# Order of the opening loads and orientation of the last expert's products in a fused attention and expert kernel

## The chip, the core and the metric

The kernel runs on one core of one Trainium2 chip. The metric is the device time of one execution in microseconds, as the median of several runs. The inputs lie in the chip's memory before the run and the output is written back to it. "fp32r" below is a float32 format that TensorE multiplies in one pass; a plain float32 product takes two.

## The reference, cut to what matters

Gated linear attention (4 sequences, 8 heads, 768 steps, head size 48), then a feed-forward layer with a rational gate (384 to 2048 to 384), then a mixture of four experts (each 384 to 1024 to 384), whose outputs are summed with normalised probabilities per token:

```python
f = 1.0 / (1.0 + np.exp(-f_logit))
for t in range(S):
    state = f[:, :, t, :, None] * state + einsum('bhd,bhe->bhde', k[:, :, t], v[:, :, t])
    y[:, :, t] = einsum('bhd,bhde->bhe', q[:, :, t], state)
...
h = x @ w_in
P = a[0] + a[1] * h + a[2] * h**2 + a[3] * h**3
Q = 1.0 + abs(b[0]) * abs(h) + abs(b[1]) * h**2
x = (P / (Q + 1e-06)) @ w_out
...
p = domain_probs / (domain_probs.sum(-1, keepdims=True) + 1e-09)
for e in range(E):
    out += p[:, e:e + 1] * (np.maximum(x @ w1[e], 0.0) @ w2[e])
```

## The kernel before, in words

Time is cut into six chunks of 128 steps. A chunk has four blocks, one per sequence, each of 128 tokens with all heads; a chunk therefore is 512 tokens. The chunks go through attention, feed-forward layer and experts as a pipeline: while TensorE multiplies chunk c by the experts' weights, the other engines prepare chunk c+1. The order on each engine is the order in which the program issues its instructions, and nothing is reordered by a scheduler.

**The opening.** `Att.start` queues, on SyncE, the loads of the first two blocks (f, k, q by `Block.load`, L415; v by `load_v`, L420) and then calls `fetch` three times. `fetch` (L726) loads one pair of raw slots: two slots of the feed-forward layer's weights, in a 64-bit format, 768 KB each. Then `Att.first(s, conv)` runs once for each s from 0 to 4. For the new block s it computes the gate sums: `exp` of f on ScalarE (L424, issued one round ahead), `w` (L428) and four `scans` on VectorE (L435), `inverse` on ScalarE, which is a logarithm and an exponential (L440, L441), then `k_hat` (L446), `newton1`, `newton2` (L451, L456) and `q_hat` (L461) on VectorE, and on TensorE `scores` (L465) and the key transposes `k_t` (L481). For the old block s-1 it runs `k_copy` (the transposed keys out of a bank on ScalarE, L485), `masked` (L476), the outputs (L489), `update` (L523), `x_hi` (L532) and `finish` (L547). In each round from s = 1 on, `conv` turns a raw slot into float32 weights: two passes on ScalarE (L738, L739), two on VectorE (L741, L742) and an addition (L745), after which the result is stored (L754) and, after every second slot, the next pair is fetched. At its end a round queues the f, k, q loads of block s+2 and the v load of block s+1; a block's tiles have two buffers, so a load waits until the block two before has been read.

**The fill.** After the fourth block the feed-forward products of chunk 0 run (`fill_in` L880, `fill_out` L887). From there on TensorE is fed without pause until the end.

**The experts.** A step v takes one slot of one expert: `mm_in` (L842) multiplies 128 hidden features by 512 tokens, nine products of 128x128 weights with 512 columns; ScalarE and VectorE split the result after the relu into a high and a low part (`gh` L950, `gl` L951); a step later `mm_out` (L852) adds the slot's share to three banks `acc`, each holding 128 features by 512 tokens, again with nine products of 512 columns. After the eight slots of an expert `evac2` multiplies the three banks by the token's probability (L987, VectorE) and adds them to the sum `o` (L988, GpSimd). A finished chunk is turned by `write_out`: for each block of 128 tokens three transposes of `o` into a bank (L1012), a copy on ScalarE (L1019) and a DMA to the output (L1021). For the last expert of the last chunk `end` does the multiplication and addition on VectorE in halves (L968, L969), then calls `write_out` for all four blocks.

Of the kernel before, what the change touches and what calls it, by code (L numbers as in the profile page):

```python
# [8 lines left out]
F32 = mybir.dt.float32  # L9
# [4 lines left out]
ALU = mybir.AluOpType  # L14
# [3 lines left out]
NB, NH, S, D = 4, 8, 768, 48  # L18
DM = NH * D
C = 128  # L20
NCH = S // C
NP = NH // 2
PR = 112
NE = 4
NJ1 = 16
NJ2 = 8
# [312 lines left out]
LAST = NCH * NE * NJ2  # L339
# [213 lines left out]
class Att:  # L553
# [24 lines left out]
    def start(self, fetch):  # L578
        nc = self.tc.nc
        for b in range(NB):  # L580
            nc.gpsimd.memset(self.st[b], 0.0)
        for b in range(2):
            blk = self.blocks[0, b] = Block(self, 0, b)
            for i in (2, 1, 0):
                blk.load(i)
            blk.load_v()
        for _ in range(3):
            fetch()

    def warm(self, n):  # L590

# [1 line left out]
        for _ in range(n):  # L593
            self.tc.nc.tensor.matmul(self.spare[:, 0:C], ident, ident, start=True, stop=True)

    def first(self, s, conv):

        new, old, nxt = (self.blocks.get((0, b)) for b in (s, s - 1, s + 1))
        rs = range(NP)
        if s == 0:  # L600
            new.exp()
            self.warm(WARM[0])
        if old:
            old.k_copy()
        if new:
            new.w()
            new.scans()
            new.inverse()
            new.k_hat()
        if nxt:  # L610
            nxt.exp()
        for f in conv[0]:
            f()
        if old:
            old.masked()
            for f in old.y_parts():
                f()
            for r in rs:
                old.update(r)
        if new:  # L620
            new.newton1()
            new.newton2()
            new.q_hat()
        if old:
            old.x_hi()
        if new:
            self.warm(WARM[1])
            for r in rs:
                new.scores(r)
            for r in rs:  # L630
                new.k_t(r)
            self.warm(WARM[2])
        for f in conv[1]:
            f()
        if old:
            old.finish()
        if s + 2 < NB:
            blk = self.blocks[0, s + 2] = Block(self, 0, s + 2)
            for i in (2, 1, 0):
                blk.load(i)  # L640
        if old and s + 1 < NB:
            self.blocks[0, s + 1].load_v()

    def loads(self, v):
        for c in range(1, NCH):
# [43 lines left out]
def fused(ctx, tc, aps, consts, gm, big, dp, prep, flag_op):  # L689


    nc = tc.nc
    w1, w2, out = aps["w1"], aps["w2"], aps["out"]
    sc, pn, ident, mask = consts

    pp = ctx.enter_context(tc.tile_pool(name="pp", bufs=1, space=PSUM))
    banks = [pp.tile([128, 512], F32, name=f"bank{i}") for i in range(8)]
    acc, hb, h1 = banks[0:3], banks[3:5], banks[5]

    def pool(name, bufs):  # L700
        return ctx.enter_context(tc.tile_pool(name=name, bufs=bufs))
# [144 lines left out]
    def mm_out(pairs, start, stop):  # L846
        for m in range(3):
            o = slice(m * 128, (m + 1) * 128)
            n, last = 0, 3 * len(pairs) - 1
            for (wh, wl), (gh, gl) in pairs:  # L850
                for a, b in ((wh, gh), (wl, gh), (wh, gl)):
                    nc.tensor.matmul(acc[m], a[:, o], b, start=(start and n == 0), stop=(stop and n == last))  # L852
                    n += 1
                    fill_step()

    def run_bounds(v):

        return (v % NJ2 == 0 or v in groups), ((v + 1) % NJ2 == 0 or v + 1 in groups)

    def emit(item):  # L860
        kind, what = item
        ts = take(len(halves(item)))
        if kind == "in2":
            c = where2(what)[0]
            mm_in(hb[what % 2], ts[0], x2[c])
        elif kind == "in1":
            c, j = what
            mm_in(h1, ts[0], att.x[c])
            gate_queue.append((c, j, h1))
        elif kind == "out2":  # L870
            mm_out([(ts[0], act2.pop(what))], *run_bounds(what))
        else:
            c, n = what
            mm_out([(ts[i], act1.pop((c, 4 * n + i))) for i in range(4)], True, True)
        make_ready(state["used"] + R)
# [85 lines left out]
    def end():  # L961

        c = NCH - 1
        for h in range(2):
            s = slice(256 * h, 256 * h + 256)
            for m in range(3):
                t = tp.tile([128, 512], F32, tag="t", name="t")
                nc.vector.tensor_tensor(out=t[:, s], in0=acc[m][:, s], in1=pb[c][:, NE - 1, s], op=ALU.mult)  # L968
                nc.vector.tensor_tensor(out=o[c][:, m, s], in0=o[c][:, m, s], in1=t[:, s], op=ALU.add)  # L969
            for b in range(2 * h, 2 * h + 2):  # L970
                write_out(c, b, banks[4 + b])

    def evac2(v):
        c, e, j = where2(v)
# [35 lines left out]
    def write_out(c, b, bank):  # L1010
        for m in range(3):
            nc.tensor.transpose(bank[:, m * C:(m + 1) * C], o[c][:, m, b * C:(b + 1) * C], ident)  # L1012
        if c < NCH - 1:
            t = osp.tile([128, DM], F32, tag="os", name="os")
        else:
            if b == 0:
                last.append(sp.tile([128, 3, 512], F32, tag="s1", name="os"))
            t = last[0].rearrange("p m t -> p (m t)")[:, b * DM:(b + 1) * DM]
        nc.scalar.copy(out=t, in_=bank[:, 0:DM])  # L1019
        r0 = b * S + c * C  # L1020
        nc.sync.dma_start(out=out[r0:r0 + C, :], in_=t)  # L1021
# [12 lines left out]
    for v in range(-FILL - 6, LAST + 1):  # L1034
        tau = v + FILL
        ops = att.begin(v)
        if tau == -4:
            prep()
        if tau + 6 <= NB:
            att.first(tau + 6, conv_ops(tau) if tau + 6 < NB else [[], []])  # L1040
        run_late()
        store_all()
        items = steps.get(v, [])
        lead = 1 if items and items[0][0] == "in2" and items[0][1] == v + 1 else 0
        fill_run(ops[PA], 9 * lead)
        for item in items[:lead]:
            emit(item)
        if 0 <= v < LAST and v not in act2:
            relu(v)
        for f in ops[ACT0]:  # L1050
            f()
        for u in gate_queue:
            if u[0] and u[:2] not in gate:
                gate[u[:2]] = gate_in(u)
        if 0 <= tau + 1 < NJ1:
            fill_in(tau + 1)
        ready = [u for u in gate_queue if u[:2] in gate]
        new = ready[0] if ready else None
        if new:
            gate_queue.remove(new)  # L1060
        old, pend_old = pend_old, new
        if new or old:
            gate_step(new, old, ops)
        else:
            for f in ops[DVE1] + ops[ACT1] + ops[POOL1]:
                f()
        c, k = v // (NE * NJ2) - 1, v % (NE * NJ2)
        if 0 <= c < NCH - 1 and k == 2:
            for b in range(2):
                write_out(c, b + (2 if c else 0), banks[6 + b])  # L1070
        fill_run(ops[PB], 9 * any(item[0] == "out2" for item in items), True)
        for item in items[lead:]:
            if item[0] == "out2":
                emit(item)
                if run_bounds(v - 1)[1]:
                    evac2(v - 1)
        for item in items[lead:]:
            if item[0] == "in2":
                emit(item)
                if v + 1 < LAST:  # L1080
                    relu(v + 1)
        if 0 <= c < NCH - 1 and k == (1 if c else 2):
            for b in range(2):
                write_out(c, b + (0 if c else 2), banks[6 + b])
        for item in items[lead:]:
            if item[0] == "out1":
                emit(item)
        for item in items[lead:]:
            if item[0] == "in1":
                emit(item)  # L1090
        for u in gate_queue:
            if not u[0] and u[:2] not in gate:
                gate[u[:2]] = gate_in(u)
        if tau == -1:
            spread_probs()
        if 0 <= tau - 2 < NJ1:
            fill_out(tau - 2)
        for f in ops[REST]:
            f()
        if v in groups:  # L1100
            evac1(*groups[v])
        if tau + 6 >= NB:
            for f in sum(conv_ops(tau), []):
                f()
            run_late()
        if 10 <= tau and v < -1:
            make_ready(min(R - 6, 2 * (tau - 9)))
            split_to(min(AHEAD, state["ready"] - 2))
        if tau == NJ1 + 1:
            for m in range(3):  # L1110
                split_x2(0, m, acc[m], nc.vector)
            load_pb(0)
        if v >= -1:
            split_to(state["used"] + AHEAD)
        att.loads(v)
        if v == 170:
            flag_op(banks[6], banks[7])
# [178 lines left out]
```

## Time and profile before

| | |
|---|---|
| median of 3 runs | 1397.06 us (1396.53 to 1398.14) |
| the profiled execution: its own time | 1395.27 us |
| the profiled execution: span on the core | 1393.5 us |
| TensorE busy, share of the span | 96% |
| VectorE, ScalarE, GpSimd busy | 64%, 48%, 21% |
| DMA, mean rate over the span | 209 GB/s |
| granted TensorE clock, mean | 0.985 of full speed |

The table says that TensorE is occupied for nearly the whole span. What is left over lies at the two ends: in the first of 40 equal slices (34.8 us each) TensorE is busy for 4 tenths, in the second for 7 tenths, in the last for 7 tenths, and in all between for 8 or 9. Times inside a profile are counted in us from the start of the span.

### The profile page before, as it was taken

The numbers are of one execution on the slowest core, as the hardware profiler recorded it, in microseconds if no ns is written. First come the engines' busy times: TensorE is split into PE (matmuls) and PEld (weight loads), VectorE is DVE, ScalarE is ACT, GpSimd is POOL, SyncE is SP. The second block draws the span as 40 slices with busy tenths as digits, with TensorE's granted clock in tenths as the row PEclk, the third lists the DMA queues.
The fourth block names the chain that finished last, engine by engine and source line by source line (L and its number), as shares of the span: only waits on it lengthen the run. The fifth ranks groups of instructions, "written<-read, shape, count | busy, mean of one in ns | idle before, by whom it ended". The sixth has DMA issues, their size and how long they took to land.

```text
span 1393.5 us, 19540 instructions
## 1 busy us (share of the span) xinstructions
PE 1335.1 (96%) x7134; PEld 1060.5 (76%) x7134; DVE 889.1 (64%) x1375; ACT 665.3 (48%) x1152; POOL 290.5 (21%) x257
## 2 busy tenths in 40 slices
PE   4799999899899999999999999999999999999997
PEld 4544787677678888877888877888888888888886
DVE  5899747697947666757666676566675556552222
ACT  3688437676626535534554435454454453431111
POOL 0133554566530010112001111001111001111010
PEclk8999999999999999999999999999999999999998
DMA  7546876667875656656755647566557566657660
GB/s 271 201 172 213 282 257 222 216 219 254 311 267 184 213 181 200 217 180 220 223 190 182 213 159 264 194 205 215 188 175 254 179 209 193 193 193 240 193 186 26
DMA packets 115704, 291.03 MB, mean 209 GB/s; under 512 B 13104, under 2 KB 28816, under 8 KB 114832
## 3 DMA queue, kind: packets, MB, share of 16 engines
q1 hardware_dynamic: 115024, 289.51, 62.8%
q8 instruction: 59, 0.97, 0.3%
q14 instruction: 45, 0.37, 0.1%
q10 hardware_dynamic: 576, 0.18, 0.1%
HBM read 240.83 MB, written 48.81 MB: 208 GB/s over the span
## 4 chain that ended last, share of the span: by engine, by line
PE 79%; DVE 13%; ACT 3%; DMA 2%; issue 1%; POOL 0%; SPq 0%; ACTq 0%; DVEq 0%; POOLq 0%
PE bank L852 36%; PE bank L842 33%; PE bank L887 3%; PE bank L880 3%; PE bank L489 2%; PE bank L465 1%; DVE q L916 1%; DVE g L435 1%; DMA f<-in_qkf_dram 1%; DVE q L925 1%; DVE y L935 1%; DVE y L937 1%; DVE q L911 1%; DVE q L913 1%; DVE gl L951 1%
## 5 line engine op out<-in xcount | busy, mean ns | idle before, releaser
L842 PE MATMUL bank<-x,w 128*128 128x512 f32 x2448 | 604.5, 394 | 11.3 <-DVE gl L951 9.1
L842 PEld LDWEIGHTS bank<-x,w 128*128 128x128 f32 x2448 | 457.3, 189 | 107.9 <-DVE gl L951 11.6
L852 PE MATMUL bank<-gh,w 128*128 128x512 f32 x1632 | 516.8, 396 | 6.6 <-DVE t L987 6.6
L852 PEld LDWEIGHTS bank<-gh,w 128*128 128x128 f32 x1632 | 302.8, 189 | 73.3 <-DVE t L987 7.4
L852 PE MATMUL bank<-gl,w 128*128 128x512 f32 x816 | 320.6, 393 | 0.0
L951 DVE SCALAR_TENSOR_TENSOR gl<-bank,gh 128x512 fp32r<-128x512 f32 x192 | 131.4, 685 | 153.0 <-ACT gh L950 152.5
L988 POOL TENSOR_TENSOR o<-o,t 128x512 f32<-128x512 f32 x69 | 89.0, 1319 | 549.4 <-DVE t L987 549.4
L852 PEld LDWEIGHTS bank<-gl,w 128*128 128x128 f32 x816 | 153.9, 189 | 33.1
L950 ACT ACTIVATE gh<-bank 128x512 fp32r<-128x512 f32 x192 | 113.6, 593 | 130.7 <-PE bank L842 130.7
L916 DVE SCALAR_TENSOR_TENSOR q<-q,sc,r 128x512 f32<-128x512 f32 x80 | 62.4, 780 | 152.3 <-ACT r L901 152.3
L799 POOL TENSOR_TENSOR w<-rawbuf,w 128x384 fp32r<-128x384 f32 x96 | 108.0, 1151 | 93.5 <-ACT w L798 77.5
L927 ACT CAST gh<-q 128x512 fp32r<-128x512 f32 x80 | 49.2, 615 | 159.0 <-DVE q L925 158.9
L896 ACT COPY h<-bank 128x512 f32<-128x512 f32 x80 | 46.8, 585 | 127.7 <-PE bank L842 127.2
L1005 DVE TENSOR_TENSOR s<-s,bank 128x512 f32<-128x512 f32 x45 | 30.6, 681 | 74.1 <-PE bank L852 74.1
L942 DVE TENSOR_TENSOR gl<-q,gh 128x512 fp32r<-128x512 f32 x80 | 56.0, 700 | 31.4 <-ACT gh L927 31.3
L917 ACT ACTIVATE r<-q,sc 128x512 f32<-128x512 f32 x80 | 58.0, 725 | 31.0 <-DVE q L916 24.2
L911 DVE SCALAR_TENSOR_TENSOR q<-q,r 128x512 f32<-128x512 f32 x80 | 65.7, 821 | 0.0
L902 ACT ACTIVATE y<-h,sc 128x512 f32<-128x512 f32 x80 | 64.2, 803 | 0.0
L435 DVE TENSOR_TENSOR_SCAN g<-f,sc 112x128 f32<-112x128 f32 x96 | 63.3, 719 | 0.5
L925 DVE SCALAR_TENSOR_TENSOR q<-y,sc,q 128x512 f32<-128x512 f32 x80 | 62.5, 781 | 1.8
L918 ACT ACTIVATE r<-r 128x512 f32<-128x512 f32 x96 | 60.8, 633 | 3.0
L937 DVE SCALAR_TENSOR_TENSOR y<-y,sc,h 128x512 f32<-128x512 f32 x80 | 60.1, 752 | 2.8
(103 smaller groups left out, 1216.4 us busy)
## 6 DMA issues: line engine op xcount, KB each, us to landing
w<-ws SPq DMA_DIRECT2D x448, 384.0 KB, 3.6
ws<-w SPq DMA_DIRECT2D x96, 384.0 KB, 4.0
raw<-in_w_dram SPq DMA_DIRECT2D x16, 768.0 KB, 6.9
rawbuf<-in_w_dram SPq DMA_DIRECT2D x64, 192.0 KB, 3.6
v<-in_v_dram SPq DMA_DIRECT2D x24, 320.0 KB, 4.7
f<-in_qkf_dram SPq DMA_DIRECT2D x24, 256.0 KB, 3.6
k<-in_qkf_dram SPq DMA_DIRECT2D x24, 256.0 KB, 4.1
q<-in_qkf_dram SPq DMA_DIRECT2D x24, 256.0 KB, 4.4
```

The costliest lines, as they stand in the source:

```text
L435: self.nc.vector.tensor_tensor_scan(g[:, r], f[:, r], lim, 1.0, ALU.mult, ALU.min)
L799: nc.gpsimd.tensor_tensor(out=t[:, 1], in0=r, in1=t[:, 0].bitcast(F32), op=ALU.subtract)
L842: nc.tensor.matmul(ps, a[:, o], b[:, kk, :], start=(n == 0), stop=(n == 8))
L852: nc.tensor.matmul(acc[m], a[:, o], b, start=(start and n == 0), stop=(stop and n == last))
L902: nc.scalar.activation(out=y, in_=h, func=AF.Identity, scale=sc[:, 0:1], bias=sc[:, 1:2])
L911: vec.scalar_tensor_tensor(out=q0, in0=q0, scalar=QC, in1=r0, op0=ALU.add, op1=ALU.mult)
L916: vec.scalar_tensor_tensor(out=q, in0=q, scalar=sc[:, 5:6], in1=r, op0=ALU.mult, op1=ALU.add)
L925: vec.scalar_tensor_tensor(out=q0, in0=y0, scalar=sc[:, 3:4], in1=q0, op0=ALU.subtract, op1=ALU.mult)
L937: vec.scalar_tensor_tensor(out=y, in0=y, scalar=sc[:, 2:3], in1=h, op0=ALU.subtract, op1=ALU.mult)
L950: nc.scalar.activation(out=gh, in_=h, func=AF.Relu)
L951: nc.vector.scalar_tensor_tensor(out=gl, in0=h, scalar=0.0, in1=gh.bitcast(F32), op0=ALU.max, op1=ALU.subtract)
L988: nc.gpsimd.tensor_tensor(out=o[c][:, m], in0=o[c][:, m], in1=t, op=ALU.add)
```

## The change

Three edits. (1) `start` fetches one pair of raw slots instead of three; the second pair is fetched at the end of round 0, behind the loads of the third block's f, k, q, and the third pair at the end of round 1, behind the fourth block's f, k, q and the third block's v. (2) In a round, `k_copy` of the old block is issued behind the new block's gate sums and `inverse` instead of ahead of them. (3) For the last expert of the last chunk the products are formed token by feature: the activations are the weights of the array, the expert's weights stream as 384 columns, and four banks hold 128 tokens by 384 features each. The sum of the first three experts is transposed and copied four and three steps before the last; at the end VectorE multiplies a bank by the probability of its tokens, adds the copied sum, and the DMA follows.

```diff
@@ start
-        for _ in range(3):
-            fetch()
+        fetch()
@@ first
-        if old:
-            old.k_copy()
         if new:
             new.w()
             new.scans()
             new.inverse()
             new.k_hat()
+        if old:
+            old.k_copy()
...
         if old and s + 1 < NB:
             self.blocks[0, s + 1].load_v()
+        if s + 2 < NB:
+            fetch()
@@ fused
     acc, hb, h1 = banks[0:3], banks[3:5], banks[5]
+    tok = acc + [h1]
...
+    def mm_tokens(w, g, start, stop):
+        (wh, wl), (gh, gl) = w, g
+        for b in range(NB):
+            o = slice(b * C, (b + 1) * C)
+            for n, (a, m) in enumerate(((gh, wh), (gh, wl), (gl, wh))):
+                nc.tensor.matmul(tok[b][:, 0:DM], a[:, o], m, start=(start and n == 0), stop=(stop and n == 2))
+                fill_step()
...
-            mm_out([(ts[0], act2.pop(what))], *run_bounds(what))
+            if what >= LAST - NJ2:
+                mm_tokens(ts[0], act2.pop(what), *run_bounds(what))
+            else:
+                mm_out([(ts[0], act2.pop(what))], *run_bounds(what))
@@ end
-        for h in range(2):
-            s = slice(256 * h, 256 * h + 256)
-            for m in range(3):
-                t = tp.tile([128, 512], F32, tag="t", name="t")
-                nc.vector.tensor_tensor(out=t[:, s], in0=acc[m][:, s], in1=pb[c][:, NE - 1, s], op=ALU.mult)
-                nc.vector.tensor_tensor(out=o[c][:, m, s], in0=o[c][:, m, s], in1=t[:, s], op=ALU.add)
-            for b in range(2 * h, 2 * h + 2):
-                write_out(c, b, banks[4 + b])
+        for b in range(NB):
+            t = last[0][:, b]
+            nc.vector.scalar_tensor_tensor(out=t, in0=tok[b][:, 0:DM], scalar=pn[:, c * NB + b, NE - 1:NE], in1=t,
+                                           op0=ALU.mult, op1=ALU.add)
+            r0 = b * S + c * C
+            nc.sync.dma_start(out=out[r0:r0 + C, :], in_=t)
@@ the loop over steps v, ahead of out2
+        if v in (LAST - 4, LAST - 3):
+            for b in range(2):
+                write_out(NCH - 1, b + 2 * (v - LAST + 4), banks[6 + b])
```

**Order on SyncE, from the first block's v load on.** `raw` are the raw slots; f, k, q and v belong to the second, third and fourth block in turn. Before:

```order
L420 DMA v<-in_v_dram 128x640
L415 DMA f<-in_qkf_dram 128x512
L415 DMA k<-in_qkf_dram 128x512
L415 DMA q<-in_qkf_dram 128x512
L420 DMA v<-in_v_dram 128x640
L726 DMA raw<-in_w_dram 128x1536 x6
L415 DMA f<-in_qkf_dram 128x512
L415 DMA k<-in_qkf_dram 128x512
L415 DMA q<-in_qkf_dram 128x512
L415 DMA f<-in_qkf_dram 128x512
```

And with the change, the same place:

```order
L728 DMA raw<-in_w_dram 128x1536 x2
L415 DMA f<-in_qkf_dram 128x512
L415 DMA k<-in_qkf_dram 128x512
L415 DMA q<-in_qkf_dram 128x512
L728 DMA raw<-in_w_dram 128x1536 x2
L415 DMA f<-in_qkf_dram 128x512
L415 DMA k<-in_qkf_dram 128x512
L415 DMA q<-in_qkf_dram 128x512
L420 DMA v<-in_v_dram 128x640
L728 DMA raw<-in_w_dram 128x1536 x2
```

Four raw loads moved from ahead of the third block's f to behind its q; two of them moved on, behind the third block's v.

**Order on ScalarE, from the second block's exponential of f to the first passes over a raw slot.** Before:

```order
L424 ACTIVATE f<-f 112x512
L485 COPY kt<-bank_98 128x448
L440 ACTIVATE r<-g 112x512
L441 ACTIVATE r<-r 112x512
L424 ACTIVATE f<-f 112x512
L738 ACTIVATE t,big<-raw 128x768
```

And with the change:

```order
L440 ACTIVATE r<-g 112x512
L441 ACTIVATE r<-r 112x512
L485 COPY kt<-bank_98 128x448
L424 ACTIVATE f<-f 112x512
L740 ACTIVATE t,big<-raw 128x768
```

The copy of the first block's keys went behind the second block's logarithm and exponential; it still stands ahead of the third block's exponential of f.

**Order on TensorE, three steps before the end.** `x` are the chunk's tokens, `gh` and `gl` the split activations, `o` the sum over the experts so far. Before:

```order
L842 MATMUL bank_96<-x_10810,w 128x512 x9
L852 MATMUL bank_92<-gh,w 128x512 x2
L852 MATMUL bank_92<-gl,w 128x512
L852 MATMUL bank_93<-gh,w 128x512 x2
L852 MATMUL bank_93<-gl,w 128x512
L852 MATMUL bank_94<-gh,w 128x512 x2
L852 MATMUL bank_94<-gl,w 128x512
```

And with the change:

```order
L844 MATMUL bank_95<-x_10810,w 128x512 x9
L1023 MATMUL bank_98<-ident,o 128x128 x3
L1023 MATMUL bank_99<-ident,o 128x128 x3
L863 MATMUL bank_92<-w,gh 128x384 x2
L863 MATMUL bank_92<-w,gl 128x384
L863 MATMUL bank_93<-w,gh 128x384 x2
L863 MATMUL bank_93<-w,gl 128x384
L863 MATMUL bank_94<-w,gh 128x384 x2
L863 MATMUL bank_94<-w,gl 128x384
L863 MATMUL bank_97<-w,gh 128x384 x2
L863 MATMUL bank_97<-w,gl 128x384
```

Nine products of 512 columns became twelve of 384, in four banks, and six of the twelve transposes that closed the kernel stand between two products here; the other six stand in the step before.

## Rows read from the trace of the kernel before

**Rows 1.** The page, busy time, share of the span and instructions of the engines.

```profile
PE 1335.1 (96%) x7134; PEld 1060.5 (76%) x7134; DVE 889.1 (64%) x1375; ACT 665.3 (48%) x1152; POOL 290.5 (21%) x257
```

**Rows 2.** Stretches of the opening: length, engines' busy us, granted clock, DMA share, GB/s.

```profile
8.00:12.00 4.00, 4.00 (x32) 3.88 (x33) 3.90 (x10) 0.63 (x1) 0.00 (x0) 1.00 1.05 392
12.00:16.00 4.00, 4.00 (x64) 3.56 (x60) 2.99 (x6) 1.69 (x3) 0.00 (x0) 1.00 1.01 421
20.00:24.00 4.00, 0.00 (x0) 0.00 (x0) 0.00 (x0) 0.16 (x1) 0.00 (x0) 0.99 1.03 389
24.00:28.00 4.00, 0.00 (x0) 0.00 (x0) 2.45 (x4) 2.93 (x6) 0.00 (x0) 0.50 0.40 149
44.00:48.00 4.00, 4.00 (x30) 3.74 (x28) 3.79 (x6) 2.10 (x5) 0.00 (x0) 0.57 0.52 207
28.00:52.00 24.00, 14.70 (x156) 13.05 (x156) 22.95 (x47) 10.09 (x18) 0.00 (x0) 0.73 0.41 144
```

**Rows 3.** The chain of waits, 0 to 30 us: start, length, what.

```profile
10.63 13.19 DMA f<-in_qkf_dram
```

**Rows 4.** The order of time on ScalarE and VectorE, second and third block.

```profile
10.38 1.37 DVE L435 TENSOR_TENSOR_SCAN g<-f,sc 112x128 f32<-112x128 f32 x4
...
12.96 0.53 ACT L485 COPY kt<-bank 128x448 f32<-128x448 f32 x1 [4.06 <-PE bank L481]
13.39 0.64 ACT L440 ACTIVATE r<-g 112x512 f32<-112x512 f32 x1
...
14.72 0.69 DVE L451 SCALAR_TENSOR_TENSOR i<-g,r 112x512 f32<-112x512 f32 x1 [1.01 <-ACT r L441]
16.17 0.69 DVE L461 TENSOR_TENSOR q<-q,i 112x512 f32<-112x512 f32 x1
...
23.84 0.63 ACT L424 ACTIVATE f<-f 112x512 f32<-112x512 f32 x1 [9.15 <-DMA f<-in_qkf_dram]
25.37 0.56 DVE L741 TENSOR_SCALAR t<-t 128x768 int32<-128x768 int32 x1 [8.51 <-ACT t L738]
```

**Rows 5.** The order of time on SyncE's queue, 6 to 14 us.

```profile
6.80 3.71 SPq L726 DMA_DIRECT2D raw<-in_w_dram  x6
10.63 0.43 SPq L415 DMA_DIRECT2D f<-in_qkf_dram  x1
12.96 0.33 SPq L415 DMA_DIRECT2D k<-in_qkf_dram  x1
```

**Rows 6.** DMA issues at 6.7 and 10 us: KB, us from issue to landing.

```profile
raw<-in_w_dram SPq DMA_DIRECT2D x1, 768.0 KB, 5.4
...
f<-in_qkf_dram SPq DMA_DIRECT2D x1, 256.0 KB, 13.2
```

**Rows 7.** The order of time on TensorE where an earlier chunk is transposed.

```profile
1261.58 0.82 PE L1012 MATMUL bank<-ident,o 128*128 128x128 f32 x6
1262.16 0.71 PE L852 MATMUL bank<-gh,w 128*128 128x512 f32 x2
```

**Rows 8.** TensorE's products and weight loads: order of time, page groups, one line's instructions.

```profile
1370.50 2.20 PE L842 MATMUL bank<-x,w 128*128 128x512 f32 x9
1372.54 0.61 PE L852 MATMUL bank<-gh,w 128*128 128x512 f32 x2
...
L842 PEld LDWEIGHTS bank<-x,w 128*128 128x128 f32 x2448 | 457.3, 189 | 107.9 <-DVE gl L951 11.6
...
L1012 PEld LDWEIGHTS bank<-ident,o x72: 137/140/230, 414.2 to 1387.0; 128*128 128x128 f32 x72
```

**Rows 9.** The order of time at the end of the kernel.

```profile
1380.70 0.62 PE L852 MATMUL bank<-gh,w 128*128 128x512 f32 x2
...
1382.52 0.40 PE L852 MATMUL bank<-gl,w 128*128 128x512 f32 x1
...
1387.70 0.48 ACT L1019 COPY os<-bank 128x384 f32<-128x384 f32 x1 [0.16 <-PE bank L1012]
```

**Rows 10.** Groups of VectorE by line, shapes apart.

```profile
L537 DVE TENSOR_TENSOR x<-bank,x 128x384 fp32r<-128x384 f32 x20 | 11.0, 548 | 0.0
```

More of the change, by code (lines that the diff above doesn't have):

```diff
@@ L594, in warm, with first @@
             self.tc.nc.tensor.matmul(self.spare[:, 0:C], ident, ident, start=True, stop=True)
-    def first(self, s, conv):
+    def first(self, s, conv, fetch):
         new, old, nxt = (self.blocks.get((0, b)) for b in (s, s - 1, s + 1))
@@ L1012, in write_out @@
             nc.tensor.transpose(bank[:, m * C:(m + 1) * C], o[c][:, m, b * C:(b + 1) * C], ident)
[L1013 to L1018, printed above, removed]
+        if c == NCH - 1:
+            if not last:
+                last.append(sp.tile([128, NB, DM], F32, tag="s1", name="os"))
+            nc.scalar.copy(out=last[0][:, b], in_=bank[:, 0:DM])
+            return
+        t = osp.tile([128, DM], F32, tag="os", name="os")
         nc.scalar.copy(out=t, in_=bank[:, 0:DM])
@@ L1039, in fused @@
         if tau + 6 <= NB:
-            att.first(tau + 6, conv_ops(tau) if tau + 6 < NB else [[], []])
+            att.first(tau + 6, conv_ops(tau) if tau + 6 < NB else [[], []], fetch)
         run_late()
```

## The prediction

> **What bounds the kernel now.** I read the page first: TensorE is busy for 96% of the span [rows 1], so only work on it, or time in which it has nothing to do, can change the time by much. The slices put what is missing at the two ends, so I looked at the opening by stretches. From 20 to 24 us no engine computes, while the DMA engines are full at 389 GB/s [rows 2]. The chain of waits names the cause: one DMA, the f of the third block, is on the chain for 13.19 us [rows 3]; ScalarE sat idle 9.15 us for it and VectorE 8.51 us behind ScalarE [rows 4]. SyncE's queue says why it is late: six raw slots are issued ahead of it [rows 5]. From 28 to 52 us VectorE works 22.95 of 24 us [rows 2], so that stretch is a chain of VectorE's instructions that starts with the late f; after it TensorE takes over to the end. At the end, the last product is over at 1382.92 us [rows 9] and the span runs on to 1393.5: 10.6 us of multiplications, transposes, copies and writes with no product beside them.
>
> **The opening loads.** Four raw loads of 768 KB, 3.15 MB, no longer stand ahead of the third block's f. The DMA engines moved 389 to 421 GB/s there [rows 2]; at 400 that is 7.9 us, and f would land not at 23.8 but at 15.9. The other bound: the first raw slot was issued at 6.80 and landed 5.4 us later, at 12.2 [rows 5, 6]. Behind it now come one more slot and f, 1.05 MB or 2.6 us: 14.8. I take 15.2, nearer to the second, which reads a load of the same short queue. SyncE issues f some 2.5 us earlier, because four issues of about 0.6 us are gone (six in 3.71 us [rows 5]).
>
> From f to VectorE: the exponential started at 23.84 and VectorE's first pass over the raw slot at 25.37, 1.53 us later [rows 4]. So this pass starts at 16.7 instead of 25.37. The floor is VectorE's own queue: `q_hat` of the second block ends at 16.86 before and, by the next edit, near 15.9. **The opening gains 8.7 us**, with 7.9 (f at 15.9) and 9.5 (the floor) as its ends.
>
> What is late next? k and q of the third block wait, as before, for the first block's key transposes and go out at 12.96 [rows 5]; the multiplication that reads k comes behind the raw slot's passes and that block's scans, and at most 1.6 MB is queued beside k, 4 us. The second raw pair goes out behind q, near 14, and is read two rounds after the first. The chain of 24 us on VectorE [rows 2] holds nearly three rounds, some 8 us each: it is read near 32, the third pair, which goes out near 20, near 40. Each has over 10 us of slack beside its 4 us of transfer, and the queue has no more bytes in total than before. Between them in SyncE's queue, the fourth block's f leaves near 15, lands by 20, and is needed a round after the third block's, near 24. The fourth block's k and q and the third block's v still wait for TensorE's reads, and the third raw pair and the first store stand behind them; neither is needed soon. TensorE's work in this stretch isn't on the chain: it waits for VectorE. So I carry the 8.7 us through to the first products and from there, TensorE being the bound, to the end.
>
> **The key copies.** On ScalarE the copy waited for TensorE until 12.96, and the logarithm behind it, whose scans had ended at 11.75, started at 13.39; VectorE waited 1.01 us for the result [rows 4]. With the copy behind, logarithm and exponential end near 13.1, the copy near 13.6, and VectorE's Newton step starts when VectorE is free, 1.0 us earlier. That is what brings the floor above to 15.9; with f at 15.2 it hides behind f, so it gets no term of its own. In the third and fourth round the logarithm waits for the scans either way. The copy then comes about 1.9 us after the scans (0.64, 0.63 and 0.53), while TensorE's `update`, which reads it, follows `k_hat` (0.69 us, the shape of `q_hat` [rows 4]), two maskings of much the same size and the outputs, some 3 us after the scans. If that cover were gone, it would cost up to 1 us a round.
>
> **The products of the last expert.** Nine products of 512 columns start 2.04 us apart from the next group [rows 8], 0.227 us each, 0.213 at 2.4 GHz being the columns and 0.013 the rest. With 384 columns that gives 0.16 + 0.013 = 0.173, or 0.170 if the rest shrinks too; twelve take 2.08 or 2.04 us. I take the dearer: 0.04 us a slot, 0.3 for seven slots (the eighth is in the tail). The fourth bank costs nothing, since the feed-forward products that use it are over by then.
>
> The twelve transposes leave the tail and stand in the stream. Six between two products took from 1261.58 to 1262.16, 0.58 us [rows 7]; twelve cost **1.2 us**. Their copies on ScalarE lie beside products that keep TensorE busy for 4 us a step.
>
> The tail: the last slot's first product starts at 1380.70 and the last copy is ready at 1388.18, 7.5 us later [rows 9]; what follows, the last write and the end of the program, 5.3 us, stays. With the change the twelfth product starts 1.9 us after the first and ends 0.35 later; VectorE's last step, 384 columns out of a bank, is like the 548 ns of [rows 10]: 2.9 us in all. The steps of the other three blocks fit between (0.52 us of products to each block). That is 4.6 us less; I allow 0.2 for four writes that now follow each other closely. **The end gains 4.4 - 1.2 - 0.3 = 2.9 us.** Its bounds: 3.3 with the cheaper product and no crowding, about 0 if a weight load of 189 ns [rows 8] with the 0.013 set the pace (0.03 us more for each of 96 products).
>
> **Sum.** 8.7 + 2.9 = 11.6 us. The profiled execution took 1395.27 us, of which 1393.5 is span, and would take 1383.7. It lies 1.8 us below the median of the runs, whose own spread is 1.6; from the median 1397.06 I forecast 1385.5.
>
> **The rivals.**
> *The f keeps its latency.* The loads issued into the full queue took about 13 us each [rows 6]. If f took 13.2 us from its new issue at 8.1, it would land at 21.3; the opening gains 2.5, the whole 5.4: 1391.7. Against it stands the first raw slot with its 5.4 us, three times as large and issued into the emptier queue. 7%.
>
> *The clock is low when the products begin.* The granted clock fell to 0.50, the 1.2 GHz level, after TensorE had idled from 20 us on, and was 0.57 from 44 to 48 us, after another idle piece [rows 2]; from 48 us on it was full. The idle pieces now lie elsewhere. If a fall of that length (3.4 us at half speed, from 0.43/0.5 of 4 us) meets the first products, it costs 1.7 to 3.4 us: 1388.0. 14%.
>
> *The shorter products run at the pace of the weight loads*, the lower bound above: 1388.4. For it: 189 ns is longer than the 160 ns of 384 columns. Against it: the transposes' loads are shown with 140 ns [rows 8], and six transposes came 0.097 apart [rows 7], so the shown length is not the spacing. 9%.
>
> *The late raw pairs take f's place.* If the second or third pair came over 10 us later than I reckon, `conv` would wait for it and the opening would gain nothing: 1394.2 to 1397. Only a queue blocked on a TensorE wait could do this, and those waits end early. 5%.
>
> *Weight loads stand in series with the products (slower).* Place: the 96 products of the last expert; price: 0.189 + 0.170 = 0.36 us each instead of 0.173, 17.9 us; with the 11.6 gained that is 6.3 slower: 1403.4. It decides from 0.295 us a product on. Against it: in series 512 columns would need 0.40 us where the row shows 0.227 [rows 8]. 3%. The Trainium skill, "TensorE: Matmul & The Clock Gate", section "The mechanism", says that a weight load overlaps products in flight only when the row group differs, which here it never does; with its load time of 128 columns at 1.2 GHz, 107 ns, I estimate 0.27 us a product, some 9 us more, and a change that is 2.6 us faster. With that rule the trace doesn't agree: by it 512 columns would need 0.32 us.
>
> **How the numbers follow.** The forecast has 62%, and the rivals in order 7, 14, 9, 5 and 3. About 0.2% (2.8 us) is what a measurement of this kernel can tell from no change: faster 0.92 (forecast and the first three), same 0.05, slower 0.03. The best case, 9.5 + 3.3 = 12.8, with the profiled execution's 1.8 below the median, gives 1382.5; I begin the range at 1382. Above, clock and weight-load pace together (1385.5 + 2.6 + 2.9) give 1391.0, and I end there; the first rival, the fourth and the fifth, 15%, stay out.
>
> **What would show it.** The third block's f lands near 15 us after an issue near 8; ScalarE's wait for it is about 1.5 us; VectorE's first pass over the raw slot starts between 15.9 and 17.5; the stretch in which VectorE is the chain ends near 43 instead of 52 us. The last expert's products start 0.17 us apart, six transposes stand in each of two steps, and the span ends 8 us after the last slot's first product. The prediction is wrong if f lands after 20 us, if a raw slot is on the chain of waits, or if these products are over 0.2 us apart.

## The result and the profile after

| | before | with the change |
|---|---|---|
| median of the runs, us | 1397.6 | 1384.88 |
| lowest to highest, us (4 runs each) | 1396.53 to 1400.29 | 1383.47 to 1386.22 |
| span of the profiled execution, us | 1393.5 | 1381.7 |
| granted TensorE clock, mean | 0.985 | 0.990 |

The ratio is 0.9907 (95% interval 0.9894 to 0.9919): faster, by 12.7 us in the medians and by 11.8 in the profiled spans. The page's first part, which answers to [rows 1]:

```profile
PE 1333.9 (97%) x7158; PEld 1062.9 (77%) x7158; DVE 885.1 (64%) x1367; ACT 665.7 (48%) x1152; POOL 290.1 (21%) x257
```

TensorE does as much work as before (24 products more) in a shorter span; what went was idle time at the ends.

**The opening.** SyncE's queue in the order of time, which answers to [rows 5] (start, length, queue, line, what):

```profile
6.37 1.30 SPq L728 DMA_DIRECT2D raw<-in_w_dram  x2
7.78 0.37 SPq L415 DMA_DIRECT2D f<-in_qkf_dram  x1
13.06 0.33 SPq L415 DMA_DIRECT2D k<-in_qkf_dram  x1
...
13.91 0.90 SPq L728 DMA_DIRECT2D raw<-in_w_dram  x2
```

The DMA issues from 6.8 to 8.8 us, KB and us to landing, which answer to [rows 6]:

```profile
raw<-in_w_dram SPq DMA_DIRECT2D x1, 768.0 KB, 6.4
f<-in_qkf_dram SPq DMA_DIRECT2D x1, 256.0 KB, 6.6
```

The third block's f leaves 2.85 us earlier and needs 6.6 us instead of 13.2: it lands at 14.4, where it landed at 23.8. ScalarE and VectorE in the order of time, which answer to [rows 4]:

```profile
11.85 0.63 ACT L440 ACTIVATE r<-g 112x512 f32<-112x512 f32 x1 [3.38 <-DVE g L435]
...
13.06 0.53 ACT L485 COPY kt<-bank 128x448 f32<-128x448 f32 x1
13.73 0.68 DVE L451 SCALAR_TENSOR_TENSOR i<-g,r 112x512 f32<-112x512 f32 x1
...
14.37 0.63 ACT L424 ACTIVATE f<-f 112x512 f32<-112x512 f32 x1 [0.77 <-DMA f<-in_qkf_dram]
...
15.17 0.69 DVE L461 TENSOR_TENSOR q<-q,i 112x512 f32<-112x512 f32 x1
...
15.72 0.20 ACT L740 ACTIVATION_READ_ACCUMULATOR t<-raw 128x1 f32 x1
...
15.96 0.56 DVE L743 TENSOR_SCALAR t<-t 128x768 int32<-128x768 int32 x1
```

VectorE's pass over the raw slot starts at 15.96 instead of 25.37, 9.41 us earlier. Two things end just before it: `q_hat`, VectorE's own work, at 15.86, and ScalarE's first pass over the slot, which stands behind f, at 15.92. So f and VectorE's own queue meet here; neither leaves the other much room. From there to the last masking of the opening, which ends at 42.7 us, VectorE shows no wait: its own queue is the limit in that stretch. The stretches between, columns as in [rows 2]:

```profile
20.00:24.00 4.00, 0.02 (x1) 0.00 (x0) 3.83 (x11) 1.52 (x3) 0.00 (x0) 1.00 0.91 307
24.00:28.00 4.00, 3.54 (x43) 3.06 (x44) 3.84 (x7) 2.89 (x6) 0.00 (x0) 0.57 0.99 399
...
52.00:56.00 4.00, 1.65 (x4) 0.38 (x2) 3.48 (x7) 4.00 (x8) 1.81 (x1) 1.00 0.26 87
56.00:60.00 4.00, 3.25 (x6) 1.49 (x7) 3.96 (x8) 3.97 (x8) 1.69 (x1) 0.77 0.97 354
60.00:64.00 4.00, 4.00 (x9) 1.66 (x8) 3.97 (x8) 3.97 (x7) 0.59 (x2) 0.80 0.37 149
```

From 20 to 24 us VectorE works 3.83 of 4 us, where nothing computed before. TensorE's idle pieces are followed by a low clock in other places than before: at 24 us, between 32 and 40 us (0.79 in both stretches), and near 58 to 62 us, after it had worked only 1.65 of 4 us. The first and the fourth group of feed-forward products, in the kernel before:

```profile
54.01 2.77 PE L880 MATMUL bank<-x,wf 128*128 128x512 f32 x6
...
66.15 2.84 PE L880 MATMUL bank<-x,wf 128*128 128x512 f32 x6 [3.09 <-DVE y L937]
```

and with the change:

```profile
44.60 2.77 PE L893 MATMUL bank<-x,wf 128*128 128x512 f32 x6
...
56.76 4.10 PE L893 MATMUL bank<-x,wf 128*128 128x512 f32 x6 [3.10 <-DVE y L950]
```

They start 9.41 and 9.39 us earlier, but the fourth runs at the low clock, 4.10 us instead of 2.84, and so does what follows to 62 us: after it 7.8 us of the gain are left (the fifth group starts at 63.70 instead of 71.47). Half a microsecond comes back in the rest of the fill. In the second chunk, from 220 to 380 us, the distance grows by another 1.1 us, and at the last expert it is 9.3 us. TensorE still waits for VectorE at places there, and the low clock lies elsewhere than before (0.84 from 260 to 280 us before, 0.91 from 250 to 270 us now); which of the two gives it back is not separated.

**The end.** TensorE's last expert in the order of time: one step, six transposes with their neighbour, and the end with VectorE (the same products before started at 1354.18):

```profile
1344.86 2.20 PE L844 MATMUL bank<-x,w 128*128 128x512 f32 x9
1346.90 0.51 PE L863 MATMUL bank<-w,gh 128*128 128x384 f32 x2
1347.24 0.34 PE L863 MATMUL bank<-w,gl 128*128 128x384 f32 x1
...
1349.00 2.24 PE L844 MATMUL bank<-x,w 128*128 128x512 f32 x9
1351.08 0.51 PE L863 MATMUL bank<-w,gh 128*128 128x384 f32 x2
...
1359.45 0.82 PE L1023 MATMUL bank<-ident,o 128*128 128x128 f32 x6
1360.03 0.59 PE L863 MATMUL bank<-w,gh 128*128 128x384 f32 x2
...
1373.32 0.51 PE L863 MATMUL bank<-w,gh 128*128 128x384 f32 x2
...
1374.04 2.19 DVE L979 SCALAR_TENSOR_TENSOR os<-bank,pn,os 128x384 f32<-128x384 f32 x4 [3.38 <-PE bank L863]
...
1375.23 0.34 PE L863 MATMUL bank<-w,gl 128*128 128x384 f32 x1
```

Two products take 0.34 us, the twelve 2.10 us (1346.90 to 1349.00), six transposes 0.58. From the last slot's first product at 1373.32 to the end of the span it is 8.4 us, where it was 12.8 (1380.70 [rows 9] to 1393.5). So the 11.8 us are 9.3 ahead of 1344.86 and 2.5 behind it.

### The profile page after: what moved, and what is told of

Read it like the earlier page. It is cut to its first block, busy times and chain, and to the rows that moved or that the text cites. A ratio compares the mean times of both kernels' runs of the same rounds, so it can differ in the third digit from the quotient of the medians.

```text
span 1381.7 us, 19576 instructions
## 1 busy us (share of the span) xinstructions
PE 1333.9 (97%) x7158; PEld 1062.9 (77%) x7158; DVE 885.1 (64%) x1367; ACT 665.7 (48%) x1152; POOL 290.1 (21%) x257
## 4 chain that ended last, share of the span: by engine, by line
## 5 line engine op out<-in xcount | busy, mean ns | idle before, releaser
L844 PEld LDWEIGHTS bank<-x,w 128*128 128x128 f32 x2448 | 456.8, 189 | 107.8 <-DVE gl L964 11.8
L854 PE MATMUL bank<-gh,w 128*128 128x512 f32 x1584 | 502.1, 397 | 5.0 <-DVE t L998 5.0
L854 PEld LDWEIGHTS bank<-gh,w 128*128 128x128 f32 x1584 | 293.9, 189 | 70.0 <-DVE t L998 6.1
L854 PE MATMUL bank<-gl,w 128*128 128x512 f32 x792 | 311.6, 393 | 0.0
L854 PEld LDWEIGHTS bank<-gl,w 128*128 128x128 f32 x792 | 149.3, 189 | 32.3
L930 ACT ACTIVATE r<-q,sc 128x512 f32<-128x512 f32 x80 | 58.0, 725 | 30.2 <-DVE q L929 23.1
```

What stands on the lines that cost most here:

```text
L844: nc.tensor.matmul(ps, a[:, o], b[:, kk, :], start=(n == 0), stop=(n == 8))
```

## The experiments

All are against the kernel before, in three groups, each with its own runs of it (medians 1396.52, 1396.73 and 1396.20). Two theories stand against each other: that late f was the opening's whole loss and the tail the rest, as predicted; or that the key copies, or the place where the clock falls, made part of it.

**The loads alone.** The kernel before with edit 1 only:

```diff
-        for _ in range(3):
-            fetch()
+        fetch()
@@ first, at the end
+        if s + 2 < NB:
+            fetch()
```

> The kernel before with the first edit alone: one pair of raw slots ahead of the third block's f, k, q, the other two pairs behind. My theory: the late f was the whole of the opening's gap; f lands near 14.4 us as in the changed kernel, but ScalarE is held by the key copy, the logarithm and the exponential until 14.7, and VectorE's q_hat of the second block ends at 16.86, so VectorE's first pass over a raw slot starts at 16.9 instead of 25.37: 8.5 us faster, near 1389. Rival: the key copies carry a good part of the opening's gain; then this gains less than 7 us and the pass starts after 18. Rival: the bytes, not the order, set the opening; then f lands after 20 and the gain is below 4 us.

Measured: 1388.03 us, ratio 0.9936 (0.9919 to 0.9953), 8.5 us less than before in the medians. ScalarE and VectorE:

```profile
14.53 0.69 DVE L451 SCALAR_TENSOR_TENSOR i<-g,r 112x512 f32<-112x512 f32 x1 [0.86 <-ACT r L441]
14.60 0.63 ACT L424 ACTIVATE f<-f 112x512 f32<-112x512 f32 x1
...
16.60 0.55 DVE L742 TENSOR_SCALAR t<-t 128x768 int32<-128x768 int32 x1
```

The exponential finds its f there; the Newton step waits 0.86 us for the logarithm behind the key copy, and the raw pass starts at 16.60, 0.64 later than with all three edits. The load order carries the opening.

**The key copies alone.** `k_copy` moved behind `k_hat`, nothing else:

```diff
-        if old:
-            old.k_copy()
...
             new.k_hat()
+        if old:
+            old.k_copy()
```

> The kernel before with the second edit alone: key copies behind the logarithm. My theory: VectorE's Newton step of the second block starts 1.0 us earlier, but f still lands near 23.8, so nothing reaches the end: within 1 us of before (1397.6), VectorE's first raw pass still near 25.4. Rival: the copy behind the logarithm helps or hurts by itself; then over 1 us either way, with update waiting for the copied keys if it hurts.

Measured: 1395.84, ratio 0.9994 (0.9983 to 1.0006), no difference that can be measured. ScalarE and VectorE:

```profile
13.85 0.68 DVE L451 SCALAR_TENSOR_TENSOR i<-g,r 112x512 f32<-112x512 f32 x1
...
23.43 0.63 ACT L424 ACTIVATE f<-f 112x512 f32<-112x512 f32 x1 [9.72 <-DMA f<-in_qkf_dram]
24.96 0.56 DVE L741 TENSOR_SCALAR t<-t 128x768 int32<-128x768 int32 x1 [8.98 <-ACT t L738]
```

The Newton step has lost its wait of 1.01 us [rows 4], and the wait behind it has grown: the time is still f's.

**The last expert alone.** The kernel before with edit 3 only (`mm_tokens`, the early `write_out` and the new `end` of the diff above).

> The kernel before with the third edit alone: the last expert token by feature. My theory: 4.4 us less behind the last slot's first product, 1.9 us more in the stream (two groups of six transposes of 0.58 us, and about 0.1 us a step for twelve products of 384 columns instead of nine of 512): 2.5 us faster, near 1395.1. Rival: the gain of this edit shows only together with the opening's (the two shift the phase of the clock and of VectorE's waits in between); then 1 us or less.

Measured: 1392.76, ratio 0.9972 (0.9959 to 0.9984), so 2.2 to 5.7 us less, 3.8 in the medians. Its profiled execution, the slowest of six, shows more than the ratio. The opening's code is that of before, yet TensorE's fourth group of products reads, in the order of time,

```profile
67.26 5.49 PE L892 MATMUL bank<-x,wf 128*128 128x512 f32 x6 [3.10 <-DVE y L949]
```

which is 1.1 us later than before and twice as long, at a granted clock of 0.50. The last expert then starts 2.8 us later than before (1357.01 against 1354.18), and the span is 0.2 longer: the end gains 2.6 us, as in the changed kernel (2.5), and the low clock under the feed-forward products took it back in this one execution.

**The change without the key copies.** Edits 1 and 3 with `k_copy` back ahead of `new.w()`, run in two groups; and the change itself run again, in the second of them and in the third.

> The changed kernel with the key copies put back ahead of the gate sums. My theory: VectorE's floor moves from 15.9 back to 16.9 us, so the first raw pass starts 0.9 to 1.0 us later and the kernel is 0.9 us slower than the changed one, near 1385.8. Rival: later stretches swallow it, and it's equal to the changed kernel within 0.3 us in span.

> The changed kernel with the key copies ahead of the gate sums, once more and beside the changed kernel itself. Theory: the copies are worth what VectorE's queue shows, 0.4 to 0.9 us. Rival: they are worth the 2 us by which the first profiles differ, of which 1.3 was a low clock that met the last block's outputs; if that was chance, it doesn't return here.

> The changed kernel unchanged, beside the three others of this group, so that they are compared on one chip: 12 to 13 us faster than before; the place of the low clock after 55 us may differ from the first profile by a few us, and with it the span by up to 2 us.

> The changed kernel once more, as the measure for the two beside it: 9 to 13 us faster than before.

| | us | ratio (95%) |
|---|---|---|
| without the key copies, first group | 1386.16 | 0.9925 (0.9908 to 0.9942) |
| without the key copies, second group | 1386.12 | 0.9922 (0.9899 to 0.9945) |
| the change, second group | 1387.64 | 0.9933 (0.9914 to 0.9952) |
| the change, third group | 1385.98 | 0.9925 (0.9911 to 0.9939) |

Side by side in the second group the key copies are worth nothing that can be measured. In the first group's profile without edit 2 the raw pass starts at 16.38 instead of 15.96, but in the second group's, also without it, at 15.99. In the seven other profiles that have edit 2 beside edit 1 it starts at 16.02 to 16.88, since VectorE waits there for ScalarE's pass behind f. The first measurement of the change, 0.9907, was the best of three; over the three it gains 9.1 to 12.7 us, and the second fell short of the 12 to 13 us expected of it. What differs between executions shows in the stretches of the change in the second group:

```profile
44.00:48.00 4.00, 4.00 (x31) 2.69 (x21) 1.78 (x4) 2.14 (x4) 0.00 (x0) 0.58 0.92 339
...
56.00:60.00 4.00, 0.90 (x2) 0.50 (x2) 3.97 (x7) 3.97 (x8) 0.52 (x1) 0.79 0.71 204
60.00:64.00 4.00, 4.00 (x6) 1.69 (x5) 4.00 (x7) 3.97 (x7) 1.83 (x1) 0.50 0.86 353
```

The clock is low at 44 to 48 us, under the first products, and again from 58 us on, under the fourth group, each time after TensorE had stood idle for VectorE. This execution begins its last expert 3.76 us behind the first one of the same code; 0.67 us of that is there at the raw pass already (16.63 instead of 15.96, since f landed later), and the first and fourth group of feed-forward products take 3.90 and 5.49 us in it instead of 2.77 and 4.10.

**The probabilities later.** `prep`, five VectorE instructions that normalise the probabilities in the third block's round, moved to the last round, where `conv` has ended:

```diff
-        if tau == -4:
-            prep()
-            att.first(tau + 6, conv_ops(tau) if tau + 6 < NB else [[], []], fetch)
+            att.first(tau + 6, conv_ops(tau) if tau + 6 < NB else [[], [prep]], fetch)
```

> The changed kernel with the five small VectorE steps that normalise the probabilities moved from the round of the third block to the round after the fourth, where VectorE idles 2.2 us. Theory: the opening is now a chain of VectorE's instructions from the first raw pass to the last masking, so every step taken out of it moves the end: 1.2 us faster than the changed kernel. Rival: the loads still set the pace; then nothing moves and a wait for a DMA appears in front of a VectorE or ScalarE step instead.

Measured: 1384.63, 0.9903 (0.9882 to 0.9925), 3.0 us under the change beside it (1387.64). VectorE's first raw passes of two rounds:

```profile
16.88 0.56 DVE L743 TENSOR_SCALAR t<-t 128x768 int32<-128x768 int32 x1 [1.15 <-ACT t L740]
...
26.05 0.55 DVE L743 TENSOR_SCALAR t<-t 128x768 int32<-128x768 int32 x1
```

They stand 9.17 us apart, where the change has 10.41 (15.96 to 26.37): 1.24 us out of a chain that is VectorE's. The rest of the 3.0 can't be told from the spread of the runs: the intervals overlap. The first products start at 44.73, against 45.82 in the change beside it, although the raw pass starts 0.25 us later (16.88 against 16.63): the shorter chain reaches them. In the first profile of the change, with f earlier and the clock full there, they start at 44.60. So VectorE bounds the opening from the first raw pass on; when that pass starts, f decides, as the wait of 1.15 us shows.

**Work of that chain on GpSimd.** On top of the last edit, `k_hat` of blocks 2 to 4 and every addition of `conv` go to GpSimd:

```diff
-        eng = self.nc.gpsimd if self.c else self.nc.vector
+        eng = self.nc.gpsimd if self.c or self.b else self.nc.vector
...
-            eng = nc.vector if CONV1[i] < NB - 6 else nc.gpsimd
+            eng = nc.gpsimd
```

> The kernel of prep_late, and also the four additions that make float32 weights of the first raw slots, and the key products of blocks two to four, on GpSimd instead of VectorE. Theory: 1.2 us as in prep_late, four additions of 0.9 us and two key products of 0.7 us leave VectorE's chain, 6 us at most; GpSimd is idle there and has 1.8 us for an addition. I expect 3 to 6 us faster than the changed kernel. Rival: ScalarE, busy 3.97 of 4 us at 32 to 36 us, takes VectorE's place, or GpSimd and VectorE slow each other down; then 2 us or less beyond prep_late.

Measured: 1384.48, 0.9912 (0.9893 to 0.9931), no better than the edit it builds on. Two additions on GpSimd, and what VectorE ran beside them:

```profile
17.72 1.80 POOL L747 TENSOR_TENSOR wf<-t 128x768 int32<-128x768 int32 x1 [4.61 <-DVE t L744]
18.24 1.57 DVE L428 TENSOR_SCALAR f<-f 112x512 f32<-112x512 f32 x1
...
36.43 2.00 POOL L747 TENSOR_TENSOR wf<-t 128x768 int32<-128x768 int32 x1 [3.67 <-DVE t L744]
36.79 2.45 DVE L744 SCALAR_TENSOR_TENSOR t<-raw,t 128x768 int32<-128x768 int32 x1
```

The addition and minimum of L428 takes 0.42 us elsewhere and 1.57 here; L744 takes 0.96 and 2.45. Both end soon after GpSimd does (19.81 after 19.52, 39.24 after 38.43), as if they had stood still until then. A third addition does the same (L428 takes 1.58 us beside it); the fourth stands beside maskings, which keep their 1.29 us. So three of the four additions give back more than the 0.96 us that each frees. The Trainium skill, "SBUF — State Buffer", section "SBUF: two separate sides", says that VectorE and GpSimd share a port pair which one holds for a whole instruction while the other blocks, where VectorE's instruction has two inputs in the SBUF or runs in a two-port mode. The rows of L744, which has two such inputs, agree; whether L428, which has one, runs in that mode no run here shows.

The expectation's first rival, ScalarE in VectorE's place, shows as well, though what ScalarE waits for is a load. ScalarE and VectorE of the same profile:

```profile
24.45 0.63 ACT L424 ACTIVATE f<-f 112x512 f32<-112x512 f32 x1 [1.36 <-DMA f<-in_qkf_dram]
...
25.98 0.56 DVE L743 TENSOR_SCALAR t<-t 128x768 int32<-128x768 int32 x1 [1.14 <-ACT t L740]
```

ScalarE is ready for the fourth block's f at 23.1 us, and it lands at 24.4. So there it is a load again that sets the pace.

**TensorE kept busy.** The change with products of the identity, whose results nobody reads, where TensorE would idle: 14, 6 and 6 more in the rounds, 2 and 11 ahead of the third and fourth group of feed-forward products:

```diff
-            self.warm(WARM[2])
+            self.warm(WARM[2] + (0, 14, 6, 6)[s])
...
+        for _ in range({1: 2, 2: 11}.get(tau, 0)):
+            nc.tensor.matmul(banks[0][:, 0:C], ident, ident, start=True, stop=True)
```

> The changed kernel with idle products of the identity in TensorE's gaps of the opening: 14 more in round 1, 6 more in rounds 2 and 3, 2 ahead of the third and 11 ahead of the fourth first-layer product of the fill, each about 0.25 us and together a little less than each gap. Theory: the changed kernel's executions differ because the granted clock falls to 0.5 after a gap, at a place that differs from one execution to the next, and now and then meets the last block's outputs and the first products; with the gaps filled the clock stays at 1.00 from 16 us on, the fourth product starts near 57 us and takes 2.8 us, and the median falls by 1 to 3 us below the changed kernel. Rival: the low clock doesn't come from the gaps; then the clock falls as before and nothing is gained.

Measured: 1383.74, 0.9912 (0.9897 to 0.9926), 2.2 us under the change beside it in the medians, with intervals that overlap. What differs clearly is the spread: its four runs lie within 0.5 us (1383.53 to 1384.07), the change's six within 4.7 (1383.73 to 1388.41). Three stretches of the opening:

```profile
20.00:24.00 4.00, 2.57 (x24) 2.38 (x22) 3.76 (x12) 1.00 (x2) 0.00 (x0) 1.00 1.04 364
...
56.00:60.00 4.00, 3.34 (x13) 1.71 (x12) 3.96 (x7) 3.97 (x7) 1.15 (x1) 1.00 1.01 334
60.00:64.00 4.00, 4.00 (x11) 1.62 (x10) 3.96 (x7) 3.97 (x9) 0.69 (x1) 1.00 0.52 212
```

The granted clock is full there, and the fourth group of products takes 2.84 us; one fall is left, from 32 to 40 us (0.84 and 0.73 in the two stretches). With the clock's falls gone from the products the spread is gone too, as the theory says, so far as one profile can stand for four runs.

**Three of them together.** Identity products, `prep` late, and `k_hat` alone on GpSimd, which runs beside a VectorE instruction that reads a bank.

> The kernel of warm_all with the probabilities normalised a round later and the key products of blocks two to four on GpSimd, but the additions of the weights left on VectorE, since GpSimd's additions stretched a VectorE step from 0.42 to 1.57 us. Theory: 1.2 us from the probabilities and 0.7 us a block for two blocks come on top of warm_all: 2 to 3 us below it. Rival: VectorE is no longer the chain, a DMA or ScalarE wait takes it; then under 1 us below it.

Measured: **1382.11**, 0.9898 (0.9884 to 0.9912), 3.9 us under the change beside it and 14.1 under the kernel before. It is 1.6 under the identity products alone, less than the 2 to 3 expected and more than the rival's 1; what `prep` and `k_hat` are each worth is not separated. Its slowest run, 1383.45, is faster than the fastest of either, 1383.73 and 1394.05. In it GpSimd's `k_hat` costs VectorE nothing:

```profile
22.08 1.29 DVE L476 TENSOR_TENSOR am<-bank,mask 128x512 f32<-128x512 f32 x2
22.18 1.28 POOL L446 TENSOR_TENSOR k<-k,g 112x512 f32<-112x512 f32 x1 [9.07 <-DVE g L435]
```

The two maskings take 1.29 us as without it. The low clock is not gone for good: in this execution, the slowest of the four, it meets the first group of products, which takes 4.18 us instead of 2.77:

```profile
43.57 4.18 PE L893 MATMUL bank<-x,wf 128*128 128x512 f32 x6
```

**What a product's weight load costs.** The change with 128 of the 384 columns streamed; the other 256 columns of this expert's output are left out:

```diff
-                nc.tensor.matmul(tok[b][:, 0:DM], a[:, o], m, start=(start and n == 0), stop=(stop and n == 2))
+                nc.tensor.matmul(tok[b][:, 0:128], a[:, o], m[:, 0:128], start=(start and n == 0), stop=(stop and n == 2))
```

> The changed kernel with the last expert's products of the last chunk streaming 128 columns instead of 384 (the other 256 columns of that expert's output are left out, so its part of the sum is missing there). It measures where weight loads set the pace. Theory: at 384 columns the columns set it (0.173 us a product), so with 128 the spacing falls to that of the loads, 0.07 to 0.12 us. Rival: loads stand in series with the columns; then 384 to 128 saves exactly 0.107 us at 2.4 GHz and leaves 0.067, with no floor. Rival: the load sets the pace already at 384; then the spacing stays above 0.16 us.

TensorE in the order of time (one run, 1380.48 us):

```profile
1349.60 0.38 PE L863 MATMUL bank<-w,gh 128*128 128x128 f32 x2
...
1349.93 0.39 PE L863 MATMUL bank<-w,gh 128*128 128x128 f32 x2
```

Three products take 0.33 us, 0.11 each, where the columns alone would be 0.053 at 2.4 GHz and 0.067 with the 0.013 of rest. So something other than the columns sets the pace of these products, near 0.11; at 384 columns, 0.173, it doesn't, and in series the two would have given 0.28 (0.11 + 0.17). That it is the weight load is argued and not shown. The Trainium skill, "TensorE: Matmul & The Clock Gate", section "LDWEIGHTS (loading the stationary operand)", says that a load of P columns takes about P/1.2 ns; for 128 columns I estimate 107 ns from that, near the 0.11. Against it stand the six transposes above, which also have 128 columns and a load each and come 0.097 us apart (0.58 for six).

## Why the prediction was right, step by step

The forecast was 1385.5; the three measurements of the change are 1384.88, 1385.98 and 1387.64, all inside its range. Against the kernel before they gain 12.7, 10.2 and 9.1 us where 11.6 was forecast: the mechanism is right, and that the first measurement lies within 0.6 us of the forecast is in part luck.

- **f behind two slots instead of six.** Right: it lands at 14.4 us in the first profile (taken: 15.2; ends 14.8 and 15.9) and between 14.1 and 15.3 in those of the other kernels with this load order. The loads alone gave 8.5 us, 8.7 predicted. The lower end was too high by 0.4 to 0.7.
- **VectorE's floor near 15.9.** Right: `q_hat` ends at 15.86, and the raw pass follows at 15.96. In the seven other profiles with edits 1 and 2 the floor hides behind f, as the prediction said. Without edit 2 the raw pass is 0.4 and 0.6 us later in two profiles and not later in a third (15.99); in the times it is worth nothing that the runs can tell.
- **The fourth block's f "lands by 20".** Wrong: it leaves at 14.91 as forecast, needs 8.8 us and lands at 23.7. Five more loads leave SyncE's queue from 18.70 us on, before it lands; whether they hold it up is not shown. It cost nothing only because ScalarE reads it at 24.06; in the run with more work on GpSimd it was late (1.36 us, above).
- **"So I carry the 8.7 us through."** Only partly right. The 9.4 us of the first products were 7.8 after the fourth group. Later stretches gave back 1.6 us, so that 9.3 us reached the last expert. In the second group's execution they gave back 1.4 us, but the clock and a later f had taken more, and 5.6 us reached it.
- **The clock rival, 14%,** was put beside the forecast as another outcome. The runs show it as the spread inside the outcome: whether the fall meets the first products, the fourth group or an idle piece differs between executions of one kernel. Its price of 1.7 to 3.4 us has the right size: the change's other two profiled executions, 3.4 and 2.6 us longer in their spans than the first, both have the low clock under the first products and the fourth group. At the raw pass a later f made 0.7 and 0.1 us of that.
- **Products of 384 columns.** 0.173 to 0.175 us and 2.10 for twelve, 0.173 and 2.08 predicted. But the nine products of 512 columns beside them also grew, from 2.04 to 2.08 a step, which the prediction had not. From the last expert's first step to the last slot's first product it is 28.46 us (1344.86 to 1373.32) instead of 26.52: 1.9 us with the transposes, where 1.5 was predicted.
- **Twelve transposes.** 0.58 us for six, both times: 1.2, as predicted.
- **The tail.** 4.4 us less, as predicted; VectorE's step takes 0.55 us (2.19 for four). The parts of the 2.9 us from the last slot's first product to VectorE's end add up to 2.8; measured are 2.9 (1373.32 to 1376.23). The end's net is 2.5 instead of 2.9.
- **Late raw pairs, an f that keeps its latency, weight loads at the pace or in series.** None of them: no raw slot is waited for, f needs half the latency, and the product pace is that of the columns.

The sum, 11.6, stands beside 11.8 in the profiled spans, with the opening 0.6 better and the end 0.4 worse than forecast.

## What to carry to other kernels

A load's latency is mostly the queue that it shares: order the opening's loads by when they are read, and check with the bytes ahead, not with the latency that the old order shows. The prediction came within about a microsecond for the third block's f and missed the fourth's by over 3 us, so look at the next load too. When the late load is gone, read what stands ready behind it, here VectorE's own queue, since the next gain is there until a load is late again. A comparison at the level of 0.2% has to ask where the clock was low in each execution before it credits an edit with the difference.

## What the runs showed of the hardware that was not expected

Two integer additions on GpSimd slowed VectorE instructions that touch only the SBUF to 1.57 and 2.45 us (0.42 and 0.96 alone), while maskings that read a bank kept their 1.29 us beside a GpSimd multiplication. Work added to an idle TensorE cut the spread of the runs from 4.7 us (six runs) to 0.5 us (four); its median is 2.2 us lower, with intervals that overlap.
